# Two MLPs cut into four products that hand over through DRAM, one of them by Strassen's algorithm

## The chip, the cores and the metric

One core of a Trainium2 chip runs the whole program. The metric is the device time of one execution in microseconds (us); three executions of the kernel before took 1062.81, 1064.90 and 1064.33 us, median 1064.33.

## The reference

Decay attention, then an MLP with swish, then an MLP with a leaky ramp, all in float32:

```python
batch, n_heads, seq, head_dim = 4, 8, 576, 64        # q, k, v: float32
scores = q @ k.T / sqrt(D) + cum[..., :, None] - cum[..., None, :]   # cum = cumsum(log f), causal
x = softmax(scores) @ v                              # -> x: 2304 tokens x 512
h = x @ w1_in;  g = h * sigmoid(1.702 * h);  y = g @ w1_out          # 512 -> 2048 -> 512
h = y @ w2_in;  g = max(h, 0) + alpha * min(h, 0);  out = g @ w2_out # 512 -> 2048 -> 512
```

The four weight matrices arrive as float64.

## The kernel before

**One core, one planner.** The kernel first lists its operations with `plan.add` (line 78): the engines that could do one, a duration for each, what it reads and writes, and a priority (a lower number goes first). `plan.run` (line 105) then walks through them in planned time, always takes the operation that can start first (among equals the one of lower priority number), gives it the engine where it ends soonest, and so writes a fixed order for TensorE (PE), VectorE (DVE), ScalarE (ACT), GpSimd (POOL) and the DMA queue on SyncE (SP). On the chip each engine works off its list in that order and waits at semaphores. A `Pool` is a set of buffers; an operation that opens a buffer waits until one is free.

**Precision.** A float32 value is split in two float32r halves, high (`a_copy`, on ACT, else on DVE) and low (`a_sub`, on POOL or DVE). A product of two such values takes three matmuls: high x high, high x low, low x high. A tile of 128 x 512 of a float64 weight becomes a float32 pair in `convert` (line 476): a 512 KB load, two ACT scalings (lines 485 and 486), then on DVE a shift (487), an `or` (490) and an addition (493), and at last the split, one copy on ACT and one subtraction (361). Three raw buffers (`wraw`) and three result buffers (`wc`) serve all weights.

**Attention** runs in 32 units: for each of 4 batches and 4 pairs of heads first the queries 0 to 255, then for all of them the queries 256 to 575. `prep` loads and transposes, `chunk` finds row maxima, `chunk2` makes the scores, the exponentials and the product with v, and writes x, transposed, into a ring `xr` of 768 tokens (line 746). Units 0 to 15 give tokens 0 to 1023, 256 for each four units, and units 16 to 31 the rest, 320 for each four.

**MLP 1, first half (`mlp1a`)** is the filler beside attention. Its priority numbers (1000 and up) stand behind attention's (100 to 131), so PE takes it when attention has nothing ready. It goes over blocks of 256 tokens in the ring, and for each over 8 of the 16 slices of the 2048 hidden columns: `mlp_slot` makes h (12 matmuls of 256 columns, line 759), tanh on ACT (765), the product on DVE (766), the split, and 12 more matmuls (line 801) add the slice to the two PSUM banks of the output. x itself and the partial output go to DRAM (`xscr`, `ypscr`).

**MLP 1, second half, and MLP 2** come after it. Five blocks of 512, 512, 512, 256 and 512 tokens are read back (`load_x`), and for each slice `mlp_slot` makes h (line 759) and 12 matmuls add it up (882 for MLP 1, 911 for MLP 2). Both products of a slice stand side by side in PE's order, so PE has a first product to do while ACT and DVE work on the slice before. The weights of a slice stay in SBUF for all blocks: 8 slots `wA` from the start, 6 slots `wB` in the space of attention once that is over, 2 slots `wC` in the space of `mlp1a`.

Of the kernel before, what the change touches and what calls it, by code (L numbers as in the profile page):

```python
# [9 lines left out]
I32 = mybir.dt.int32  # L10
# [172 lines left out]
def kernel(  # L183
# [24 lines left out]
    NA = 8  # L208
# [4 lines left out]
    NB = NM - NA  # L213
    NB1 = 6
    RING = 768
    BLK = 256
    SPLIT = 256

# [8 lines left out]
    xscr = dram.tile([P, KT, NT], F32, name="xscr")  # L227
    ypscr = dram.tile([P, KT, NT], F32, name="ypscr")
# [4 lines left out]
    def open_region(name, side, closes=()):  # L233
        if name not in region:
            for c in closes:
# [19 lines left out]
    open_region("res", "left")
    open_region("m1a", "left")
    open_region("att", "right")


    wA = sb("res", "wA", NA, [P, 2, 2 * KT, P], F32R)  # L260
    p_raw8 = sb("res", "wraw", 3, [P, 4, P, 2], I32)
    p_wc = sb("res", "wc", 3, [P, 4, P])
    p_xh = sb("m1a", "xh", 3, [P, 2, BLK], F32R)
    p_xl = sb("m1a", "xl", 2, [P, 2, BLK], F32R)
    p_g = {n: sb("m1a", n, 2, [P, BLK], d) for n, d in (("gg", F32), ("gh", F32R), ("gl", F32R))}
    p_yp = sb("m1a", "yp", 1, [P, 2, BLK])
    xr = region["m1a"][1].tile([P, KT, RING], F32, name="xr")
    m1a_pools = [p_xh, p_xl, p_yp, *p_g.values()]
# [703 lines left out]
```

## Time and profile before

| | us |
|---|---|
| median of three executions | 1064.33 (1062.81 to 1064.90) |
| span of the profiled execution, first to last instruction | 1063.1 |
| PE busy with matmuls in it | 1032.3 |
| DVE, ACT, POOL busy | 680.9, 433.3, 129.3 |
| moved by DMA | 86.54 MB, 81 GB/s in the mean |

The profiled execution has no time of its own beside the span; the span is 0.1% under the median. PE's matmuls overlap their neighbours in the records, so a single one reads longer than the step from one start to the next; the same holds for DVE's operations. In the rows, PEld is the loading of PE's weights, and PEclk the clock that was granted to PE as a share of 2.4 GHz.

### The profile page before, as it was taken

What the parts mean: (1) busy time and instruction counts of PE and PEld (TensorE: products, weight loads), DVE (VectorE), ACT (ScalarE), POOL (GpSimd) and SP (SyncE); (2) the same over time, 40 slices, a digit from 0 to 9 for tenths busy, and PEclk for the clock granted to TensorE, in tenths of its full rate; (3) what the DMA queues carried; (4) which work ended last, traced back from release to release, by engine and by line L of the source; (5) the groups of instructions that cost most, each with busy time, mean ns of one, the idle gap of its engine ahead of it and who ended that gap; (6) DMA issues with size and microseconds to landing.
All of it is one profiled execution on the core that took longest, in us unless ns stands there. A gap on an engine that the chain in (4) does not pass through costs nothing.

```text
span 1063.1 us, 17696 instructions
## 1 busy us (share of the span) xinstructions
PE 1032.3 (97%) x6563; PEld 886.8 (83%) x6563; DVE 680.9 (64%) x1523; ACT 433.3 (41%) x970; POOL 129.3 (12%) x202
## 2 busy tenths in 40 slices
PE   5888999999999999999999999999999999999998
PEld 3667888999888989998888988888888888898886
DVE  6879888887888868939953459634343533544433
ACT  4556545555556546748732348301211211211111
POOL 5222312131113010001200101100000000000000
PEclk8789999999999999999999999999999999999999
DMA  5666664332322114616751236300200100010001
GB/s 113 136 164 189 140 135 90 68 75 55 81 44 55 43 33 154 216 47 197 246 152 60 93 106 190 108 1 1 70 1 1 70 1 0 21 40 21 1 1 39
DMA packets 170055, 86.54 MB, mean 81 GB/s; under 512 B 127440, under 2 KB 155280, under 8 KB 169968
## 3 DMA queue, kind: packets, MB, share of 16 engines
q1 hardware_dynamic: 159632, 84.16, 29.1%
q10 hardware_dynamic: 10336, 1.25, 0.7%
q8 instruction: 51, 0.84, 0.3%
q14 instruction: 36, 0.29, 0.1%
HBM read 66.34 MB, written 19.02 MB: 80 GB/s over the span
## 4 chain that ended last, share of the span: by engine, by line
PE 89%; DMA 3%; DVE 3%; POOL 1%; ACT 1%; issue 1%; SPq 0%; ACTq 0%; DVEq 0%; POOLq 0%
PE bk L759 36%; PE bk L911 18%; PE bk L882 9%; PE bk L801 9%; PE bk L667 5%; PE bk L716 4%; PE bk L604 2%; DMA wraw<-in_moe_w_in_dram 2%; PE bk L687 2%; PE bk L693 1%; DMA wraw<-in_moe_w_out_dram 1%; PE bk L630 1%; DMA rq<-in_q_dram 1%; PE bk L597 1%; DVE wraw L490 0%
## 5 line engine op out<-in xcount | busy, mean ns | idle before, releaser
L356 ACT CAST qgh<-qgg 128x512 fp32r<-128x512 f32 (+1 forms) x118 | 68.3, 579 | 332.5 <-DVE qgg L773 297.1
L770 DVE TENSOR_SCALAR qgg<-bk,alpha_sb 128x512 f32<-128x512 f32 (+1 forms) x80 | 55.4, 695 | 164.9 <-PE bk L759 164.9
L759 PE MATMUL bk<-qx,wB 128*128 128x512 f32 (+1 forms) x720 | 155.5, 368 | 0.0
L759 PEld LDWEIGHTS bk<-qx,wB 128*128 128x128 f32 x720 | 126.0, 189 | 22.7
L759 PE MATMUL bk<-xh,wA 128*128 128x256 f32 x576 | 124.1, 295 | 0.0
L361 DVE TENSOR_TENSOR qgl<-qgg,qgh 128x512 fp32r<-128x512 f32 (+1 forms) x117 | 75.9, 650 | 68.8 <-ACT qgh L356 52.2
L759 PE MATMUL bk<-qx,wA 128*128 128x512 f32 (+1 forms) x480 | 103.6, 368 | 0.0
L759 PEld LDWEIGHTS bk<-xh,wA 128*128 128x128 f32 x576 | 96.7, 194 | 7.3 <-issue 3.7
L759 PEld LDWEIGHTS bk<-qx,wA 128*128 128x128 f32 x480 | 84.2, 188 | 15.3
L801 PE MATMUL bk<-gh,wA 128*128 128x256 f32 x576 | 83.7, 289 | 8.1 <-ACT gh L356 8.1
L613 DVE CUSTOM_DVE_ANT_0 bk<-bk,mask 128x512 f32<-128x512 f32 (+3 forms) x160 | 75.5, 491 | 15.5 <-PE bk L604 12.7
L801 PEld LDWEIGHTS bk<-gh,wA 128*128 128x128 f32 x576 | 74.9, 193 | 10.8 <-ACT gh L356 9.1
L759 PE MATMUL bk<-xl,wA 128*128 128x256 f32 x288 | 82.4, 286 | 0.0
L671 ACT ACTIVATE e<-bk 128x320 f32<-128x320 f32 (+3 forms) x224 | 64.9, 364 | 30.8 <-PE bk L667 26.6
L911 PE MATMUL bk<-wA,qgh 128*128 128x512 f32 x288 | 71.9, 389 | 0.0
L911 PEld LDWEIGHTS bk<-wA,qgh 128*128 128x128 f32 x288 | 53.8, 188 | 11.0
L759 PEld LDWEIGHTS bk<-xl,wA 128*128 128x128 f32 x288 | 55.9, 194 | 0.0
L882 PE MATMUL bk<-qgh,wB 128*128 128x512 f32 (+1 forms) x240 | 54.5, 369 | 0.0
L675 POOL TENSOR_SCALAR_AFFINE_SELECT e<-e 128x256 f32<-128x256 f32 (+1 forms) x80 | 34.4, 444 | 162.0 <-ACT e L671 137.0
L911 PE MATMUL bk<-wB,qgh 128*128 128x512 f32 x216 | 54.0, 390 | 0.0
L759 PE MATMUL bk<-qx,wC 128*128 128x512 f32 (+1 forms) x240 | 52.7, 368 | 0.0
L485 ACT ACTIVATE wc<-wraw 128x512 f32<-128x512 f32 x64 | 43.0, 676 | 23.0 <-DMA wraw<-in_moe_w_in_dram 14.5
(156 smaller groups left out, 1991.1 us busy)
## 6 DMA issues: line engine op xcount, KB each, us to landing
wraw<-in_moe_w_in_dram SPq DMA_DIRECT2D x32, 512.0 KB
wraw<-in_moe_w_out_dram SPq DMA_DIRECT2D x32, 512.0 KB
xscr<-xr SPq DMA_DIRECT2D x9, 512.0 KB
ypscr<-yp SPq DMA_DIRECT2D x18, 256.0 KB
rk<-in_k_dram SPq DMA_DIRECT2D x64, 72.0 KB
VR<-in_v_dram SPq DMA_DIRECT2D x32, 128.0 KB
qxb<-xscr SPq DMA_DIRECT2D x16, 256.0 KB
qyp<-ypscr SPq DMA_DIRECT2D x16, 256.0 KB
```

The source lines that it names most:

```text
L356: nc.scalar.copy(dst, src)
L361: E[e].tensor_tensor(dst, a, b, op=ALU.subtract)
L485: plan.add([("ACT", c_act(n))], lambda e: nc.scalar.mul(w.ap, high().bitcast(F32), 2.0 ** -112), [raw], [w], pri)
L613: plan.add([("DVE", c_dve(c1 - c0) + 90.0)], lambda e, pm=pm, c0=c0, c1=c1, mk=mk, m0=m0, col=col: nc.vector.tensor_tensor_reduce(pm.ap[:, ...
L667: nc.tensor.matmul(pss[hh].ap[:w, :m], x.ap[r, a:a + w], y.ap[r, s0 - q0:n], start=i == 0, stop=i == 3)
L671: plan.add([("ACT", c_act(m, True))], lambda e, hh=hh, pss=pss, e32=e32, w=w, m=m: nc.scalar.activation(e32.ap[:w, hh, :m], pss[hh].ap[:w, ...
L716: nc.tensor.matmul(pb[hh].ap[:l.shape[1], s0 - q0:n], l, rhs.ap[:w, hh, :m], start=st, stop=sp, skip_group_check=True,)
L759: nc.tensor.matmul(ph.ap[:, :n], wb.ap[:, a, c, :], x(c), start=(c == 0 and i == 0), stop=(c == KT - 1 and i == 2))
L770: plan.add([("DVE", c_dve(n) + 56)], lambda e: nc.vector.tensor_scalar(g.ap[:, :n], ph.ap[:, :n], 0.0, alpha_sb[:, m:m + 1], op0=ALU.min, ...
L801: nc.tensor.matmul(py[d // 2].ap[:, d % 2 * BLK:(d % 2 + 1) * BLK], W1[m].ap[:, a, KT + d, :], g.ap, start=(m == 0 and i == 0 and a == 0 a ...
L882: nc.tensor.matmul(py[d].ap[:, :n], W1[m].ap[:, a, KT + d, :], g.ap[:, :n], start=(m == NA and i_ == 0 and a == 0), stop=(m == NM - 1 and ...
L911: nc.tensor.matmul(py[t].ap, g.ap[:, t * P:(t + 1) * P], wo[:, a, KT * P:], start=(m == 0 and i_ == 0 and a == 0), stop=(m == NM - 1 and i ...
```

## The change

All of MLP 1's first product now runs beside attention (`gemm1`): blocks of 256 (three) and 384 tokens (four), all 16 slices each, 12 matmuls a slice; h is copied out of PSUM and stored to DRAM (`h1scr`) with no activation. The partial output and the copy of x in DRAM are gone.

The second stage reads h back in tiles of 128 x 512 (`stream`: load, tanh on ACT, product on DVE, split) and multiplies it by `w1_out`; y goes to DRAM. The third stage is MLP 2's first product. `group_x` reads y for 768 tokens as a 2 x 2 grid (two halves of the 512 inputs, two halves of 384 tokens), forms four sums of them and splits seven operands; the weights get the same treatment for each pair of slices (m, m + 8). `pair` then makes seven block products of 6 matmuls of 384 columns, where the plain way has eight; sums of products are made in PSUM by PE, and with three copies on ACT and three additions on DVE a pair. h goes to DRAM (`h2scr`) with no activation. The sums go over three groups of tokens with the first four pairs, then over the three again with the last four. The fourth stage streams h back with the leaky ramp and multiplies by `w2_out`.

SBUF regions are opened in turn: buffers of a later stage wait until all buffers of an earlier one in the same place are released (`order_of`). The 11 first slices of `w1_out` and the stream buffers take the place of attention; the other five and six slots for Strassen weights take the place of stage 1; the operands of stage 3 take the place of `w1_out`.

```diff
+    BLKS = (256, 256, 256, 384, 384, 384, 384)
+    BW = max(BLKS)
+    XH = 384
+    GRP = 2 * XH
+    NPAIR = NM // 2
+    WO0 = 11
...
+    order_of = {
+        "res": ("left", (), ()), "p1": ("left", (), ()), "att": ("right", (), ()),
+        "str": ("right", ("att",), ()), "wo0": ("right", (), ("str",)), "x0": ("right", ("wo0",), ()),
+        "ws": ("left", ("p1",), ()), "wo1": ("left", (), ("ws",)), "x1": ("left", ("wo1",), ()),
+    }
...
+    wA = sb("p1", "wA", NM, [P, 2, KT, P], F32R)
+    p_xh = sb("p1", "xh", 3, [P, 2, BW], F32R)
+    p_xl = sb("p1", "xl", 2, [P, 2, BW], F32R)
+    p_gg = sb("p1", "gg", 3, [P, BW])
...
+    p_str = {n: sb("str", n, w, [P, 512], d, att_pools) for n, w, d in (("qr", 3, F32), ("qg", 2, F32), ("qh", 3, F32R), ("ql", 2, F32R))}
+    p_yo = sb("str", "yo", 2, [P, 512], F32, att_pools)
+    wo = (sb("wo0", "woa", WO0, [P, 2, 512], F32R, att_pools), sb("wo1", "wob", NM - WO0, [P, 2, 512], F32R, p1_pools))
+    wS = sb("ws", "wS", 6, [P, WSLOT], F32R, p1_pools)
+    p_tt = sb("ws", "tt", 1, [P, 4, 2, P], F32, p1_pools)
+    p_ba = sb("x0", "ba", 6, [P, 2, XH], F32, [wo[0]])
+    p_xs = (sb("x0", "xsa", 3, [P, 2, 2, XH], F32R, [wo[0]]), sb("x1", "xsb", 4, [P, 2, 2, XH], F32R, [wo[1]]))
+    p_t = {n: sb("x1", n, 2, [P, XH], F32, [wo[1]]) for n in ("c1", "u2", "c5")}
+    p_go = sb("x1", "go", 4, [P, XH], F32, [wo[1]])
...
+    def gemm1(i, pri, vpri):
+        t0, n = starts[i], BLKS[i]
...
+        for m in range(NM):
+            ph = Buf(ps_h)
+            w = WI[m]
+
+            def hmm(e, ph, w, c0):
+                for c in (c0, c0 + 1):
+                    for j, (a, x) in enumerate(((0, xh), (0, xl), (1, xh))):
+                        nc.tensor.matmul(ph.ap[:, :n], w.ap[:, a, c, :], x[c // 2].ap[:, c % 2, :n], start=(c == 0 and j == 0), stop=(c == KT - 1 and j == 2))
+
+            for c0 in range(0, KT, 2):
+                plan.add([("PE", 6 * c_mm(n))], lambda e, ph=ph, w=w, c0=c0: hmm(e, ph, w, c0), [(w, (0, 0)), (w, (0, 1)), xh[c0 // 2], xl[c0 // 2]], [ph], pri)
+            g = Buf(p_gg)
+            plan.add(a_out(n), lambda e, g=g, ph=ph: copy(e, g.ap[:, :n], ph.ap[:, :n]), [ph], [g], vpri)
+            plan.add(DMA(P * n * 4), lambda e, g=g, m=m: nc.sync.dma_start(h1scr[:, m, t0:t0 + n], g.ap[:, :n]), [g], [(b_g1, (i, m))], vpri)
...
+            for m in range(NM):
+                WI[m] = Buf(wA)
+                pri = A0 + 4 + m * 0.3
+                w = exact(in_rows(w1_in, m), pri, A0 + 1 + m / 2 if m < 4 else None, WLAG)
+                halves(KT * P, lambda w=w: flat(w.ap), [w], lambda m=m: flat(WI[m].ap[:, 0]), lambda m=m: flat(WI[m].ap[:, 1]), WI[m], 0, pri)
...
+    def stream(src, rd, k, t0, n, act, pri):
+        raw, g, h, lo = (Buf(p_str[x]) for x in ("qr", "qg", "qh", "ql"))
+        plan.add(DMA(P * n * 4), lambda e: nc.sync.dma_start(raw.ap[:, :n], src[:, k, t0:t0 + n]), rd, [raw], pri)
+        if act == "swish":
+            plan.add([("ACT", c_act(n))], lambda e: nc.scalar.activation(g.ap[:, :n], raw.ap[:, :n], AF.Tanh, scale=0.851), [raw], [g], pri)
+            plan.add([("DVE", c_dve(n), 0.0, True)], lambda e: nc.vector.scalar_tensor_tensor(
+                g.ap[:, :n], g.ap[:, :n], 1.0, raw.ap[:, :n], op0=ALU.add, op1=ALU.mult
+            ), [raw], [g], pri)
+        else:
+            plan.add([("DVE", c_dve(n, True) + 56, 0.0, True)], lambda e: nc.vector.tensor_scalar(
+                g.ap[:, :n], raw.ap[:, :n], 0.0, alpha_sb[:, k:k + 1], op0=ALU.min, op1=ALU.mult
+            ), [raw, b_alpha], [g], pri)
+            plan.add([("DVE", c_dve(n), 0.0, True)], lambda e: nc.vector.scalar_tensor_tensor(
+                g.ap[:, :n], raw.ap[:, :n], 0.0, g.ap[:, :n], op0=ALU.max, op1=ALU.add
+            ), [raw], [g], pri)
+        plan.add(a_copy(n), lambda e: copy(e, h.ap[:, :n], g.ap[:, :n]), [g], [h], pri)
+        plan.add(a_sub(n), lambda e: sub(e, lo.ap[:, :n], g.ap[:, :n], h.ap[:, :n].bitcast(F32)), [g, h], [lo], pri)
+        return h, lo
...
+    in_turn = blocks[:-2] + [blocks[-1], blocks[-2]]
+    groups = [(t0, GRP) for t0 in range(0, NT, GRP)]
...
+    for i, (t0, n) in enumerate(in_turn):
+        base = 2000.0 + 100 * i
+        py = [Buf(ps_y) for _ in range(KT)]
+        for k in range(NM):
+            h, lo = stream(h1scr, [(b_g1, (j, k)) for j in crossing(t0, n, p1_parts)], k, t0, n, "swish", base + k - 60)
+            last = k == NM - 1
...
+            rw = [(WO[k], (0, 0)), (WO[k], (0, 1))]
+            for ds in ([d] for d in range(KT)) if last else (range(KT),):
+                pd = [py[d] for d in ds]
+                plan.add([("PE", 2 * len(ds) * c_mm(n))], lambda e, ymm=ymm, ds=ds: ymm(e, ds, ((0, 0), (1, 0))), [*rw, h], pd, base + k)
+                plan.add([("PE", len(ds) * c_mm(n))], lambda e, ymm=ymm, ds=ds: ymm(e, ds, ((0, 1),)), [*rw, lo], pd, base + k)
...
+        diff(0, cut(0)[1], cut(0)[0], w)
+        diff(1, cut(2)[1], t_(0), [w[1], (tt, 0)])
+        diff(2, cut(2)[1], cut(0)[1], [w[1]])
+        diff(3, cut(2)[0], t_(1), [w[0], (tt, 1)])
...
+        o = {}
+        o[1] = operand(a["11"], p_xs[0])
+        comb(s1, a["21"], a["22"], ALU.add)
+        comb(s2, s1, a["11"], ALU.subtract)
+        o[6] = operand(s2, p_xs[0])
+        o[2] = operand(a["12"], p_xs[0])
+        o[5] = operand(s1, p_xs[1])
+        comb(a["21"], a["11"], a["21"], ALU.subtract)
+        o[7] = operand(a["21"], p_xs[1])
+        comb(s2, a["12"], s2, ALU.subtract)
+        o[3] = operand(s2, p_xs[1])
+        o[4] = operand(a["22"], p_xs[1])
+        return o
...
+        product(1, x[1], p, ba, True, pri)
+        cp(c1, ba)
+        product(6, x[6], p, bb, True, pri)
+        add(bb, bb, c1)
+        product(2, x[2], p, ba, False, pri)
+        cp(u2, bb)
+        cp(o11, ba, a_out(XH))
+        store(o11, p, gi, 0, t0, vp)
+        product(5, x[5], p, bd, True, pri)
+        cp(c5, bd)
+        product(7, x[7], p, bb, False, pri)
+        add(o22, bb, c5)
+        store(o22, p + NPAIR, gi, 1, t0, vp)
+        product(3, x[3], p, bd, False, pri)
+        add(o12, bd, u2)
+        store(o12, p + NPAIR, gi, 0, t0, vp)
+        product(4, x[4], p, bb, False, pri)
+        cp(o21, bb, a_out(XH))
+        store(o21, p, gi, 1, t0, vp)
...
+    n_it = 0
+    for half in range(2):
+        for gi, (t0, _) in enumerate(groups):
+            base = 6000.0 + 100 * n_it
+            x = group_x(t0, base - 150)
+            for p in range(half * NPAIR // 2, (half + 1) * NPAIR // 2):
+                pair(p, x, gi, t0, base + p)
+            n_it += 1
...
+        if k % 3 == 0:
+            sw = Buf(wS)
+        W2[k] = (sw, k % 3)
+        pri = 8000.0 + k
```

Here `exact` is `convert` without the split, `halves` the split, `a_out` the copy out of PSUM on ACT or DVE, `p_ba`, `p_xs` the buffers of `group_x`, and `ps_t` six PSUM banks, three for a pair.

## Rows read from the trace of the kernel before

**Rows 1.** The page's first part: busy us, share of the span, instructions.

```profile
PE 1032.3 (97%) x6563; PEld 886.8 (83%) x6563; DVE 680.9 (64%) x1523; ACT 433.3 (41%) x970; POOL 129.3 (12%) x202
```

**Rows 2.** Stretches, all engines: length, busy us (instructions), PEclk, DMA share, GB/s.

```profile
0.00:125.00 125.00, 100.24 (x789) 80.32 (x789) 101.67 (x320) 71.20 (x173) 42.44 (x89) 0.86 0.63 149
125.00:407.00 282.00, 281.14 (x2499) 250.66 (x2495) 228.75 (x605) 149.74 (x403) 57.54 (x91) 1.00 0.32 68
407.00:467.30 60.30, 60.11 (x500) 59.91 (x500) 46.88 (x100) 39.60 (x88) 0.74 (x1) 1.00 0.55 175
467.30:680.00 212.70, 212.70 (x1028) 179.49 (x1028) 150.41 (x260) 113.82 (x203) 23.23 (x16) 1.00 0.46 145
680.00:1058.20 378.20, 378.12 (x1758) 316.47 (x1756) 153.23 (x241) 58.44 (x104) 5.35 (x5) 1.00 0.05 17
1058.20:1063.10 4.90, 0.00 (x0) 0.00 (x0) 0.00 (x0) 0.54 (x1) 0.00 (x0) 0.93 0.65 200
```

**Rows 3.** The chain that ended last, 420 to 530 us: start, us, what.

```profile
433.41 5.22 DMA wraw<-in_moe_w_in_dram
...
444.25 8.64 PE bk L759 x72
...
512.35 9.52 PE bk L759 x42
```

**Rows 4.** Waits of PE, 0 to 125 us: total us, times, longest.

```profile
PE bk L801 <- ACT gh L356: 7.9, 4, 4.1
```

**Rows 5.** Stretches, line 746 alone: DVE's writes into the ring.

```profile
0.00:226.00 226.00, 10.49 (x24) 0.92 0.55 125
```

**Rows 6.** Stretches, line 801 alone: PE, PEld.

```profile
0.00:226.00 226.00, 43.91 (x288) 38.20 (x288) 0.92 0.55 125
0.00:407.00 407.00, 84.81 (x583) 75.30 (x584) 0.96 0.41 93
```

**Rows 7.** Stretches, line 759 alone: PE, PEld.

```profile
0.00:226.00 226.00, 51.34 (x336) 44.86 (x336) 0.92 0.55 125
0.00:407.00 407.00, 97.24 (x648) 84.67 (x648) 0.96 0.41 93
```

**Rows 8.** Groups by line and shape: busy us, mean ns, idle before.

```profile
L485 ACT ACTIVATE wc<-wraw 128x512 f32<-128x512 f32 x64 | 43.0, 676 | 23.0 <-DMA wraw<-in_moe_w_in_dram 14.5 <-DMA wraw<-in_moe_w_out_dram 6.5 <-DVE wc L487 1.0
...
L766 DVE SCALAR_TENSOR_TENSOR gg<-gg,bk 128x256 f32<-128x256 f32 x72 | 29.7, 412 | 5.3 <-ACT gg L765 4.9
...
L765 ACT ACTIVATE gg<-bk 128x256 f32<-128x256 f32 x72 | 27.5, 382 | 32.8 <-PE bk L759 19.5 <-DVE gl L361 10.3 <-POOL gl L361 2.2
```

**Rows 9.** Instructions in order of time, DVE, 500 to 502 us: start, us.

```profile
499.98 0.69 DVE L490 SCALAR_TENSOR_TENSOR wraw<-wraw 128x512 int32<-128x512 int32 x1
500.58 0.69 DVE L361 TENSOR_TENSOR wA<-wc,wA 128x512 fp32r<-128x512 f32 x1
501.18 0.69 DVE L493 CUSTOM_DVE_ANT_0 wc<-wraw,wc 128x1024 uint16<-128x1024 uint16 x1
501.78 0.43 DVE L487 TENSOR_SCALAR wc<-wc 128x512 int32<-128x512 int32 x1
502.12 0.69 DVE L490 SCALAR_TENSOR_TENSOR wraw<-wraw 128x512 int32<-128x512 int32 x1
```

**Rows 10.** Instructions in order of time, all engines, 557 to 560 us.

```profile
557.55 0.60 ACT L765 ACTIVATE qgg<-bk 128x512 f32<-128x512 f32 x1 [3.98 <-PE bk L759]
...
559.56 0.69 DVE L361 TENSOR_TENSOR qgl<-qgg,qgh 128x512 fp32r<-128x512 f32 x1 [0.69 <-ACT qgh L356]
```

**Rows 11.** A stretch of 55 us, all engines, columns as in rows 2.

```profile
475.00:530.00 55.00, 55.00 (x244) 45.27 (x243) 54.29 (x92) 43.73 (x78) 9.32 (x6) 1.00 0.65 205
```

**Rows 12.** The page's second part: what all DMAs moved.

```profile
DMA packets 170055, 86.54 MB, mean 81 GB/s; under 512 B 127440, under 2 KB 155280, under 8 KB 169968
```

**Rows 13.** Instructions in order of time, the end of the span.

```profile
1057.18 0.33 SPq L931 DMA_DIRECT2D out_dram<-qyp  x1
...
1059.45 0.40 SPq L931 DMA_DIRECT2D out_dram<-qxb  x1
```

More of the change, by code (lines that the diff above doesn't have):

```diff
@@ L780, in mlp1a @@
[L780 to L784 removed]
+    b_g1, b_y1, b_g2 = Buf(), Buf(), Buf()
+    WI = {}
+    starts = [sum(BLKS[:i]) for i in range(len(BLKS))]
+    def gemm1(i, pri, vpri):
+        t0, n = starts[i], BLKS[i]
+        r0 = t0 % RING
+        xb = xr[:, :, r0:r0 + n]
+        cols = [j % (RING // 64) for j in range(t0 // 64, (t0 + n) // 64)]
@@ L830, with advance @@
+    done = {"i": 0}
+    def advance(t):
+        while done["i"] < len(BLKS) and starts[done["i"]] + BLKS[done["i"]] <= t:
+            gemm1(done["i"], 1000.0 + done["i"], -1.0)
+            done["i"] += 1
     seq = [(b, hp, q0, q1) for q0, q1 in ((0, SPLIT), (SPLIT, S)) for b in range(B) for hp in range(NP)]
@@ L840 @@
             chunk2(x)
-            advance(t, 0)
+            advance(t)
     for x, t in pend:
         chunk2(x)
-        advance(t, 0)
-    for m in range(NA, NM):
-        W1[m] = weight(wB if m < NA + NB1 else wC, w1_in, w1_out, m, 2000.0 + m)
-    blocks = []
-    for n in (512, 512, 512, NT % 512, 512):
-        blocks.append((sum(x[1] for x in blocks), n))
-    nx = {"i": 0}
+        advance(t)
     def row_of(x):
@@ new lines, in crossing @@
+    def crossing(t0, n, parts):
+        return [i for i, (a, w) in enumerate(parts) if a < t0 + n and t0 < a + w]
+    p1_parts = list(zip(starts, BLKS))
+    blocks = [(512 * i, min(512, NT - 512 * i)) for i in range((NT + 511) // 512)]
+    in_turn = blocks[:-2] + [blocks[-1], blocks[-2]]
+    groups = [(t0, GRP) for t0 in range(0, NT, GRP)]
+    WO = {}
+    for k in range(NM):
+        WO[k] = wb = Buf(wo[k // WO0])
+        pri = 1500.0 + k
+        w = exact(out_rows(w1_out, k), pri)
+        halves(KT * P, lambda w=w: flat(w.ap), [w], lambda wb=wb: wb.ap[:, 0], lambda wb=wb: wb.ap[:, 1], wb, 0, pri)
@@ new lines, with product, mm @@
+    TIDX = {1: 0, 2: 1, 3: 2, 4: 6, 5: 3, 6: 4, 7: 5}
+    def product(j, x, p, out, st, pri):
+        def mm(e):
+            t = TIDX[j]
+            w = TS[p].ap.rearrange("p (a q c n) -> p a q c n", a=2, q=7, c=2)
+            for c in range(2):
+                for i, (a, b) in enumerate(((0, 0), (0, 1), (1, 0))):
+                    nc.tensor.matmul(
+                        out.ap[:, :XH], w[:, a, t, c, :], x.ap[:, b, c, :],
+                        start=(st and c == 0 and i == 0), stop=(c == 1 and i == 2), skip_group_check=True,
+                    )
+        k = PART[TIDX[j]]
+        plan.add([("PE", 6 * c_mm(XH))], mm, [(TS[p], (k, 0)), (TS[p], (k, 1)), (x, (0, 0)), (x, (0, 1))], [out], pri)
```

287 lines of the change are left out of this document (123 added, 164 removed).

## The prediction

> **What bounds the kernel now.** The page's first part puts PE busy for 1032.3 of 1063.1 us [rows 1]; DVE, the next, has 64%. A busy PE can hide waits, so the second look is the span cut into stretches [rows 2]. The reader is to see three things there. Up to 125 us PE is busy for 100.24 us: 24.8 us are idle, and its clock is granted at 0.86. From 125 us, through the rest of attention (to about 407 us), the rest of MLP 1's first half (to 467.3 us) and everything behind it, PE is idle for 1.1 us in 933 us. The end without PE takes 4.9 us.
>
> The third look is the chain that ended last. In a full stretch it gives the true step of a matmul: 72 of 256 columns took 8.64 us, so 120.0 ns; 42 of 512 columns took 9.52 us, so 226.7 ns [rows 3]. That is a line, N / 2.4 + 13.3 ns, and 384 columns, which the kernel before does not have, come to 173.3 ns between the two. With these steps the products from 467.3 us on need 768 x 226.7 + 192 x 120 = 197.1 us (second half of MLP 1), 197.1 us (MLP 2, first product) and 864 x 226.7 = 195.9 us (second), together 590.1 us; the stretch is 590.9 us long. So the kernel is bound by PE's count of columns, and any change is read as: matmuls removed, less the places where PE has nothing ready.
>
> **The change part by part: what PE no longer does.** Stage 1: before, 9 blocks x 8 slices x 24 matmuls of 256, 1728 x 120.0 = 207.4 us. After, 192 matmuls for each of three blocks of 256 and four of 384: 192 x (3 x 120.0 + 4 x 173.3) = 202.2 us: -5.2 us, the fixed 13.3 ns of fewer matmuls. Stages 2 and 4 have the old shapes: 0. Stage 3: 3 groups x 8 pairs x 7 products x 6 = 1008 matmuls of 384, 174.7 us for 197.1: -22.4 us. In all -27.6 us.
>
> The Trainium skill has another fixed part: in "TensorE: Matmul & The Clock Gate", "Wait — 56ns, not 53.3ns?", the step is N / 2.4 GHz plus about 2.5 ns. By that the sum would be -1.0 for stage 1 and -22.9 us for stage 3, -23.9 us and 1054.4 us at the end. The chain here reads 120.0 and 226.7 ns, so the measurement decides.
>
> **Stage 1.** What it adds on PE is nothing; the question is whether attention always finds filler beside it. Before, when unit 20 was done (24 writes into the ring, 226 us), PE had done 288 + 336 filler matmuls [rows 5 to 7], 74.9 us. After, until then only three blocks are there, 576 x 120 = 69.1 us. PE would lack 5.8 us of work. Against it, DVE loses 29.7 us of products and the subtractions behind them, and ACT trades 27.5 us of tanh and as much of copies for 112 copies out of PSUM, 0.38 us for 256 columns by line 765 and for 384 some 0.5, between that and line 485's 0.676 for 512 [rows 8]; two PSUM banks that the output held are free. Attention may reach unit 20 earlier by that. In the first 125 us PE waited 7.9 us for the split of an activation [rows 4]; that wait is gone, but the same place then waits for weights, which come through the same loads and as many conversions (16 tiles either way). I take +3 for missing filler (bounds 0 and 8), -2 for the early wait (bounds -8 and 0): +1 us. At attention's end 1728 - 583 - 648 = 497 filler matmuls, 60 us, were left [rows 6, 7]; after it is at least the last block, 33 us, in which the first 11 slices of w1_out are converted.
>
> The queue: 27 stores leave SP, 112 come in, each waiting for a copy out of PSUM; at about 0.4 us to issue [rows 13] 45 us of SP's 400. Behind a late store stand loads of q, k and v, which run two units ahead. DMA in all goes from 86.5 MB [rows 12] by -18.9 (x and partial output, out and back) +75.5 (h, 2304 x 2048 x 4 bytes, twice out and back) +4.7 (y read twice) to about 148 MB. The first 125 us have a DMA share of 0.63 already [rows 2]; beside attention the stores come to +9.4 MB in 407 us, 23 GB/s, by the ratio of rows 11 (205 GB/s at 0.65) a share of 0.07. I cost it at nothing; it shows if the share nears 1.
>
> **Stage 2.** Now each slice is 12 matmuls, 2.72 us, and PE has no other product to turn to: behind the matmul that waits for `qh` stand only later slices, which come through the same buffers. Uncontended, the way from tanh to the low half took 2.70 us (557.55 to 560.25, [rows 10]); two `qg` buffers make that 1.35 us a slice. Beside it run conversions: five slices of w1_out (waiting until the buffers of stage 1 are released) and six of eight Strassen weights. DVE's real step is what the starts say, 0.60 us for 512 columns with two inputs and 0.34 for the shift, not the 0.69 in the records [rows 9]. A slice takes 1.20 us of DVE; a tile's conversion 1.54, its split 0.60. A Strassen pair: 2 x 1.54, four differences of 256 columns at about 0.34, subtractions of 512, 256 and 1024 columns at 0.60, 0.34 and 1.2, 6.6 us. The stage has 72 x 1.20 + 5 x 2.14 + 6 x 6.6 = 137 us of DVE for 197 us of PE; ACT, with two scalings of 0.676 us a tile, has less. The nearest row is the stretch from 475 to 530 us: DVE busy 54.29 of 55.00 us with conversions, PE without a gap [rows 11]. But there PE had two products to choose from. So I take +2 us for the start of the stage (bounds 0 and 5) and +3 for the conversions beside the streams (bounds 0 and 34, below).
>
> **Into stage 3 and through it.** The loads of y for group 0 wait for the buffers of slice 10 of the last block: 5 x 2.72 = 13.6 us before the stage's end. 1.57 MB at the 205 GB/s of rows 11 need 7.7 us, and a 512 KB load took 5.2 us to land [rows 3]; three operands are split by then, four after the last slice, each by one copy and one subtraction of 768 columns, which PE covers with 3.1 us of the first three products: +2 us (bounds 0 and 5). Inside a pair product 2 waits for copy c1 under cover of product 6 (1.04 us against some 0.5 us of copy and a hand-over), product 7 for an addition and a copy under products 2 and 5, product 4 for an addition under product 3; three more banks let the next pair in. In the 29 us of four pairs DVE has 11 operations of 768 columns at 0.9 us and 12 of 384 at 0.45 (from rows 9, by columns), 15 us, and ACT 7 copies of 768 at 0.9 and 20 of 384 at 0.5, 16 us. +2 us (bounds 0 and 8).
>
> **Stage 4 and the end.** Two of the six slots for w2_out come free halfway through stage 3, the others 22, 15, 7 and 0 us before its end, so ten conversions crowd around the border: +2 us (bounds 0 and 6). At the end there are two output buffers where four served. Before, the last three copies did not wait; the last DMA was issued at 1059.45 and landed by 1063.1, 3.2 us after its 0.40 us of issue [rows 13]. After, the third copy waits for the first store and the fourth for the second: about 1060.4 and 1061 us in these times, then 0.6 us, issue and 3.2 us: +2 us (bounds 0 and 3.5).
>
> **The sum.** -27.6 + 1 + 2 + 3 + 2 + 2 + 2 + 2 = -13.6 us. Against the profiled execution's 1063.1 us that is 1049.5; against the median of 1064.33, 0.1% above that execution, 1050.7 us, which I forecast.
>
> **Rivals.**
> *Everything hides.* The five inner borders cost nothing, the early wait goes by 3 us or more, only the tail stays: -27.6 - 2 + 2 us, 1036.7 us. For it: PE lost 1.1 us in 933 under the same planner. Against it: that order always held a second product.
> *The streams of stage 2 set its pace (slower).* Place: PE's wait for `qh` or `ql` in stage 2, with DVE or ACT ahead of it at Strassen conversions. Two buffers keep up while the way from tanh to low half stays under 5.44 us, so each of its four steps may wait 0.68 us, a bit more than one conversion operation. If it is 6.4 us in all 72 slices, a slice takes 3.2 us: +34 us in place of 3, 1050.7 + 31 = 1081.7 us. It turns the change into a loss from 2.95 us a slice (72 x 0.23 = 16.6 us). For it: conversions are taken whenever an engine is free, and rows 11 show DVE full by them. Against it: DVE's 137 us for the stage.
> *Filler runs out in earnest.* Blocks of 384 come later than blocks of 256, and with attention no faster PE lacks its 8 us at each of two borders, the DRAM traffic delays loads: +17 us in stage 1, 1066 us. For it: rows 5 to 7. Against it: the lack at unit 20 is 5.8 us, and each block behind it brings 33 us of filler.
>
> **How the numbers follow.** The forecast (1040 to 1062) has 0.55, everything hidden 0.21, the slow streams 0.19, the filler 0.05. A difference of 0.2%, 2.1 us, is about what a measurement of this kernel can tell. Of the slow streams 0.04 ends within it and 0.15 above; of the filler 0.02 and, below it, 0.03. Faster: 0.55 + 0.21 + 0.03 = 0.79; same 0.06; slower 0.15. The likeliest case alone spans 1040 to 1062 us. The range goes from 1034 (all hidden, with a little more of the early wait) to 1068 us, into the slow streams, and leaves out some 0.14 above and 0.04 below.
>
> **What would show it.** 1008 matmuls in stage 3 at steps of 173 ns and a stage of 177 us; stage 2 at 197 to 202 us; attention's end with 33 to 80 us of filler left; PE's waits in stage 2 named for `qh` and `ql`, around 5 us in all; a last DMA that lands some 7 us after the last matmul. Wrong it would be if PE were idle for over 15 us in one of the stages, or if a 384-column step were not near 173 ns.

## The result, and the profile after

The changed kernel took 1049.41 us (median of four executions, 1046.55 to 1054.58) beside 1063.57 for the kernel before: ratio 0.9871, 95% interval 0.9834 to 0.9907. With five further executions the median of nine is 1049.0. The forecast was 1050.7. The profiled execution is the longest of the nine, 1054.58 us with a span of 1052.8, so each stage is also read from later profiles.

Page of the changed kernel, first part, and what its DMAs moved (answers to [rows 1] and [rows 12]):

```profile
PE 1005.4 (95%) x6227; PEld 887.9 (84%) x6227; DVE 751.8 (71%) x1595; ACT 542.2 (52%) x1152; POOL 106.1 (10%) x174
...
DMA packets 211293, 147.94 MB, mean 141 GB/s; under 512 B 132320, under 2 KB 186272, under 8 KB 211200
```

Its stretches, columns as in [rows 2]: the first 125 us, the rest of stage 1, stage 2, stage 3, stage 4, the tail.

```profile
0.00:125.00 125.00, 93.99 (x767) 74.83 (x769) 97.81 (x304) 69.60 (x172) 36.51 (x82) 0.88 0.64 150
125.00:470.33 345.33, 340.93 (x2641) 309.72 (x2640) 232.95 (x578) 181.40 (x453) 46.90 (x77) 0.99 0.42 111
470.33:666.10 195.77, 195.52 (x953) 165.47 (x952) 151.61 (x269) 127.96 (x228) 0.00 (x0) 1.00 0.53 164
666.10:852.03 185.93, 180.57 (x1018) 177.62 (x1017) 136.97 (x213) 110.45 (x209) 19.97 (x13) 0.99 0.60 195
852.03:1046.89 194.86, 194.35 (x857) 160.29 (x855) 132.43 (x233) 51.64 (x90) 2.67 (x3) 1.00 0.37 110
1046.89:1052.80 5.91, 0.03 (x1) 0.00 (x0) 0.00 (x0) 1.17 (x2) 0.00 (x0) 0.92 0.48 145
```

Where PE was idle before, it is idle still, and more: 31.0 us of the first 125 for 24.8 [rows 2]. New are 4.4 idle us in the rest of stage 1 (1.05 before) and 5.4 in stage 3 (180.57 busy of 185.93). Those of stage 1 lie early; behind 170 us it is full:

```profile
170.00:470.33 300.33, 299.48 (x2273) 273.91 (x2272) 202.34 (x479) 160.81 (x391) 35.62 (x59) 1.00 0.40 111
```

Stages 2 and 4, whose streams I feared, are full. The chain that ended last (start, us, what) has 300 matmuls of 384 columns in one piece, and PE's instructions within it show six at a time:

```profile
671.50 52.38 PE bk L967 x300
```

```profile
673.69 1.20 PE L967 MATMUL bk<-xsa,wS 128*128 128x384 f32 x6
674.73 1.20 PE L967 MATMUL bk<-xsb,wS 128*128 128x384 f32 x6
675.77 1.20 PE L967 MATMUL bk<-xsa,wS 128*128 128x384 f32 x6
```

From start to start six take 1.04 us, so 173.3 ns a step, as I had it between the two steps of [rows 3]. 52.38 / 300 = 174.6 ns is a mean with small gaps in it.

PE's waits in the first 125 us (line and what it waited for; total us, times, longest), the answer to [rows 4]:

```profile
PE bk L680 <- ACT DQ L653: 9.5, 5, 5.3
...
PE bk L790 <- ACT wA L361: 4.5, 2, 2.4
...
PE bk L790 <- DVE wA L366: 1.3, 4, 0.7
```

The wait of 7.9 us for a split activation is gone; 5.8 us for weights stand in its place. The wait for `DQ`, a scaling on ACT in the attention, has grown. Before it was:

```profile
PE bk L667 <- ACT DQ L640: 2.8, 3, 2.0
```

What held the longest of the five, in order of time at 55 to 61 us:

```profile
55.52 0.50 SPq L796 DMA_DIRECT2D h1scr<-gg  x1
...
56.58 0.48 SPq L796 DMA_DIRECT2D h1scr<-gg  x1
...
60.10 0.37 ACT L361 COPY gg<-bk 128x256 f32<-128x256 f32 x1 [3.83 <-DMA h1scr<-gg]
60.37 0.38 ACT L653 ACTIVATE DQ<-bk 67x256 fp32r<-67x256 f32 x1
...
60.80 0.58 PE L680 MATMUL bk<-DQ,DK 64*128 64x256 f32 x2 [5.27 <-ACT DQ L653]
```

The copy of a new h slice waits 3.83 us until an older store has landed and its `gg` buffer is free. `DQ` stands behind the copy in ACT's order, and PE waits 5.27 us for `DQ`. An issue is 0.5 us on SP's row; the store itself is not in that record. The Trainium skill ("Perfetto Trace Analysis", "Per-instruction lifecycle: what the profiler-reported window actually captures") says that of a DMA the data movement lies outside the reported window, and that DVE and ACT work strictly in order. The rows agree: a store of 0.5 us on SP's row holds the copy for 3.83 us, and `DQ` starts only behind it.

### The profile page after: what moved, and what is told of

Same layout as the page of the kernel before. It is cut to its first block, busy times and chain, and to the rows that moved or that the text cites. A ratio compares the mean times of both kernels' runs of the same rounds, so it can differ in the third digit from the quotient of the medians.

```text
span 1052.8 us, 18331 instructions
## 1 busy us (share of the span) xinstructions
PE 1005.4 (95%) x6227; PEld 887.9 (84%) x6227; DVE 751.8 (71%) x1595; ACT 542.2 (52%) x1152; POOL 106.1 (10%) x174
## 4 chain that ended last, share of the span: by engine, by line
PE 69%; DVE 9%; DMA 3%; issue 2%; ACT 1%; SPq 0%; DVEq 0%; ACTq 0%
PE bk L1045 18%; PE bk L790 16%; PE bk L967 13%; PE bk L877 11%; PE bk L680 4%; PE bk L729 4%; DVE ql L366 1%; PE bk L617 1%; DVE qg L836 1%; DMA ba<-y1scr 1%; PE bk L706 1%; DVE wS L366 1%; DVE wc L500 1%; DMA wraw<-in_moe_w_in_dram 1%; PE bk L700 1%
## 5 line engine op out<-in xcount | busy, mean ns | idle before, releaser
L790 PE MATMUL bk<-xh,wA 128*128 128x384 f32 (+1 forms) x896 | 228.7, 326 | 6.1 <-ACT wA L361 4.5
L361 ACT CAST qh<-qg 128x512 fp32r<-128x512 f32 (+1 forms) x159 | 91.9, 579 | 169.3 <-DVE qg L843 115.8
L366 DVE TENSOR_TENSOR ql<-qg,qh 128x512 fp32r<-128x512 f32 (+1 forms) x158 | 100.5, 637 | 101.9 <-PE bk L877 48.6
L1045 PE MATMUL bk<-wS,qh 128*128 128x512 f32 x576 | 145.9, 389 | 0.5 <-ACT qh L361 0.5
L790 PE MATMUL bk<-xl,wA 128*128 128x384 f32 (+1 forms) x448 | 142.0, 317 | 0.8 <-DVE xl L366 0.8
L1045 PEld LDWEIGHTS bk<-wS,qh 128*128 128x128 f32 x576 | 108.0, 188 | 23.3 <-ACT qh L361 0.9
L967 PE MATMUL bk<-xsb,wS 128*128 128x384 f32 x576 | 110.1, 339 | 5.4 <-DVE go L989 4.0
L967 PEld LDWEIGHTS bk<-xsb,wS 128*128 128x128 f32 x576 | 101.6, 190 | 7.9 <-DVE go L989 5.3
L877 PE MATMUL bk<-qh,woa 128*128 128x512 f32 (+1 forms) x440 | 99.4, 368 | 0.0
L967 PE MATMUL bk<-xsa,wS 128*128 128x384 f32 x432 | 82.5, 334 | 0.0
```

What stands on the lines that cost most here:

```text
L361: nc.scalar.copy(dst, src)
L366: E[e].tensor_tensor(dst, a, b, op=ALU.subtract)
L790: nc.tensor.matmul(ph.ap[:, :n], w.ap[:, a, c, :], x[c // 2].ap[:, c % 2, :n], start=(c == 0 and j == 0), stop=(c == KT - 1 and j == 2))
L877: nc.tensor.matmul(py[d].ap[:, :n], w[:, a, d * P:(d + 1) * P], (lo if x else h).ap[:, :n], start=(k == 0 and (a, x) == (0, 0)), stop=(k = ...
L967: nc.tensor.matmul(out.ap[:, :XH], w[:, a, t, c, :], x.ap[:, b, c, :], start=(st and c == 0 and i == 0), stop=(c == 1 and i == 2), skip_gr ...
L1045: nc.tensor.matmul(py[t].ap, (lo if x else h).ap[:, t * P:(t + 1) * P], w[:, a], start=(k == 0 and (a, x) == (0, 0)), stop=(k == NM - 1 an ...
```

## The experiments

Differences are against the 1049.0 us of the changed kernel. Executions of one kernel differ by 2 to 9 us in all of them, and by 4 to 7 us in the kernel before; the first experiment shows where a part of it is from.

**The same kernel again.**

> The changed kernel once more. Its four executions so far run from 1046.55 to 1054.58 us, and the profiled one is the longest of them. If the loss of stage 1 in that profile (PE idle for 31.0 us in the first 125 us against 24.8 before, DQ waits of 9.5 us) belongs to the kernel, a second profile shows it again, at 29 to 33 us. If it came by chance from the timing of DMAs in that one execution, the second profile has 25 to 28 us there and a span near 1047.

1049.02 us (1046.91 to 1052.52), ratio 0.9858 (0.9837 to 0.9880). Idle in the first 125 us: 28.0 us, between both cases, and `DQ` 9.6 us again. Stage 1 ended at 470.33 once more. Six profiles (this pair and the four runs below marked *) have the same order of work through stage 1. It ended at 466.83, 467.23 and 467.23 us in three and at 470.33, 470.33 and 471.03 in the others. Two of them side by side, by the starts of `DQ` on ACT:

| | 16th `DQ` | 17th | last | stage 1 ends |
|---|---|---|---|---|
| changed kernel | 151.74 | 169.44 | 391.38 | 470.33 |
| eight products* | 150.50 | 166.18 | 388.13 | 466.83 |

From the 17th to the last `DQ` the two run in step, 3.3 us apart. So this scatter is decided before 170 us. In the rows just ahead of the 17th, ACT's copy of v waits for a late load (2.6 us in the changed kernel, 2.1 in the other) with the exponentials behind it, and PE waits for those. What carries the difference, by the rows, is PE's clock. The second measurement and the run on the tail below (first and second line) start that copy of v at 156.54 and 156.37 us and are 3.1 us apart at the 17th `DQ` (169.23 and 166.11). Their stretches from 125 to 170 us:

```profile
125.00:170.00 45.00, 40.92 (x359) 35.18 (x356) 30.22 (x96) 20.34 (x61) 11.27 (x18) 0.92 0.55 110
```

```profile
125.00:170.00 45.00, 41.52 (x399) 35.66 (x398) 32.00 (x106) 22.14 (x66) 11.30 (x18) 1.00 0.58 116
```

PE is idle for 4.1 and 3.5 us, but its clock is granted at 0.92 in the one and 1.00 in the other. In all three that end late it is 0.92, in the three that end early 0.96, 0.96 and 1.00. In the changed kernel the row of PE after that wait, and the stretch behind it at 0.50 of 2.4 GHz:

```profile
157.68 0.52 PE L680 MATMUL bk<-QH,KH 64*128 64x192 f32 x1 [2.32 <-ACT e L684]
```

```profile
158.00:162.00 4.00, 4.00 (x25) 3.54 (x24) 2.29 (x8) 2.61 (x7) 1.36 (x4) 0.50 0.71 131
```

So a wait of some 2 us can be paid twice, once in idle time and once in slower matmuls behind it; after 2.09 us in the run on the tail it was not.

**Strassen's price and gain*.**

```diff
         product(1, x[1], p, ba, True, pri)
+        product(1, x[1], p, ba, True, pri)
```

> Strassen undone in its price alone: the first block product of every pair is issued twice, the second time over the first (start=True), so stage 3 has eight products where the changed kernel has seven; everything else and the result stay. 24 pairs x 6 matmuls x 174.6 ns = 25.1 us. Theory (PE's columns set the time, what else stage 3 does is hidden): +24 to +26 us on the changed kernel, about 1073 us. Rival (stage 3 is partly set by the additions, the copies and the loads of y on DVE, ACT and DMA, so PE has slack there): +10 to +20 us, since the second product fills the 9 us that PE lost in stage 3.

1070.36 us: +21.4, between the two theories; ratio to the kernel before 1.006 (1.004 to 1.0079), so with the eighth product in place nothing of the gain is left. Stage 3 of this kernel:

```profile
662.10:867.03 204.93, 203.92 (x1166) 202.10 (x1165) 139.86 (x222) 110.73 (x206) 15.12 (x9) 1.00 0.55 177
```

Take the 1152 matmuls of eight products at the mean of 174.6 ns (201.1 us) and the 12 of stage 4 that run inside it at 226.7 (2.7 us) off the 204.93: 1.1 us lost. The same sum for seven products, with 8 of stage 4, is 185.93 - 176.0 - 1.8 = 8.1 us lost, and 5.5 in the second profile (183.33 us). So leaving out one product of eight takes 25.1 us of columns away, and PE gives some 4 to 7 us of them back (8.1 or 5.5 less 1.1 by the stage; 25.1 - 21.4 = 3.7 by the medians). That fits copies, additions and loads having an eighth less PE time to hide behind; that this is all of it is not shown.

**A fourth buffer for the stores of stage 1.**

```diff
-    p_gg = sb("p1", "gg", 3, [P, BW])
+    p_gg = sb("p1", "gg", 4, [P, BW])
```

> One more buffer (four for three) between the copy out of PSUM and the h1 store of stage 1. Theory: stage 1 lost about 6 us of its gain because the copy waits on ACT for an old store to land (3.8 us at 55.6 us of the profile) and attention's DQ scaling stands behind it in ACT's order (PE waits 5.3 us): PE's idle time in the first 125 us falls from 31.0 us to 25 to 28, the time by 3 to 5 us. Rival (the loss belongs to SP's queue, full of issues and late for q, k and v, or to the weights of the first block): idle time 30 us or more, no gain over 1 us.

1044.84 us (1043.49 to 1046.39), -4.2, as expected; but not where expected. No copy waits for a store any more, yet PE's idle time in the first 125 us is 33.0 us; between 125 us and the end of stage 1 (466.13) it is 1.3 us for 4.4, and the granted clock from 125 to 170 us is 1.00 for 0.92. One profile does not prove that place, as the scatter above is as large; and the interval (0.9798 to 0.9838) just meets that of the changed kernel's second measurement (0.9837 to 0.9880).

**Stores of two slices.**

```diff
-    p_gg = sb("p1", "gg", 3, [P, BW])
+    p_gg = sb("p1", "gg", 2, [P, 2, BW])
...
+            if m % 2:
+                plan.add(DMA(2 * P * n * 4), lambda e, g=g, m=m: nc.sync.dma_start(h1scr[:, m - 1:m + 1, t0:t0 + n], g.ap[:, :, :n]), [g], [(b_g1, (i, m - 1)), (b_g1, (i, m))], vpri)
```

> The h1 stores of stage 1 go out for two slices at a time: 56 DMAs where the changed kernel issues 112, the same bytes, two buffers of two slices (four slices in flight where three were). Theory (the copies wait for buffers whose stores are late, and SP's list is full of issues in the first 175 us): as with the fourth buffer, no wait of a copy for a store is left, and SP has 24 issues fewer in its full stretch, so 1043 to 1046 us against 1049 for the changed kernel. Rival (the issues themselves set it, not the buffer): below 1043, clearly faster than the fourth buffer's 1044.84. Second rival (each store waits for two slices, so buffers come back later): 1047 or more.

1043.73 us (1040.78 to 1046.86), -5.3: within the first theory and, at 0.9806 (0.9783 to 0.9829), clear of the changed kernel, but not to be told from the fourth buffer. ACT's waits for DMAs up to 180 us, first the changed kernel, then this one:

```profile
ACT DQ L653 <- DMA rq<-in_q_dram: 4.8, 1, 4.8
...
ACT gg L361 <- DMA h1scr<-gg: 3.8, 1, 3.8
...
ACT VH L361 <- DMA VR<-in_v_dram: 2.6, 1, 2.6
ACT VH L361 <- DMA rq<-in_q_dram: 2.5, 1, 2.5
```

```profile
ACT VH L361 <- DMA VR<-in_v_dram: 0.7, 1, 0.7
ACT VH L361 <- DMA rk<-in_k_dram: 0.5, 1, 0.5
```

Left out are the weight loads (16.5 and 19.4 us together) and one wait of `xr` of 5.5 and 5.6 us. The waits for stores are gone, and those for v are 1.2 us for 5.1. The bytes are the same, and the DMA share of the first 125 us is higher, 0.68 for 0.64, so bandwidth was hardly the lack. The granted clock from 125 to 170 us is 1.00. Stage 1 ended at 460.83 us, and at 462.73 and 463.33 in the two joined kernels below, 5.5 to 8 us before the mean of the six (468.8).

**Every store twice.**

```diff
+            plan.add(DMA(P * n * 4), lambda e, g=g, m=m: nc.sync.dma_start(h1b[:, m, t0:t0 + n], g.ap[:, :n]), [g], (), vpri)
```

> Every h1 store of stage 1 is issued twice, the second time into a DRAM tensor that nobody reads: 112 DMAs and 18.9 MB more in 470 us. Theory (stores cost stage 1 by their buffers and their place in SP's list): each buffer is held longer and loads of q, k, v stand behind more issues, stage 1 ends 4 to 12 us later, 1053 to 1061 us. Rival (what I predicted: queue and DMA traffic of the stores cost nothing): within 2 us of the changed kernel's 1049.

1052.89 us (1051.05 to 1053.55), +3.9: a shade under the theory's range and over the rival's. Copies wait for stores eight times, 10.7 us in all, for twice and 6.1 us. But the end of stage 1, expected 4 to 12 us later, is 471.7 us with 12 matmuls of stage 2 done for 8, 2 us behind the mean of the six, and the interval (0.9873 to 0.9906) just meets that of the second measurement. With half the issues 5.3 us less, with twice as many 3.9 more: the stores have a price, which the first of the two shows and the second bears out, and I had put it at nothing.

**Nine blocks of 256.**

```diff
-    BLKS = (256, 256, 256, 384, 384, 384, 384)
+    BLKS = (256,) * 9
```

> Stage 1 goes over nine blocks of 256 tokens in place of three of 256 and four of 384: 1728 matmuls for 1344, 144 stores for 112. Theory (the block size is worth its fixed part, 207.4 - 202.2 = 5.2 us, and filler did not run out with 384): +5 to +8 us, the part above 5.2 for 32 more stores, 1054 to 1057 us. Rival (blocks of 384 come too late as filler beside attention, which cost what their matmuls gained): within 2 us of the changed kernel, 1047 to 1051.

1058.28 us (1056.01 to 1062.44), +9.3. More than the 5.2 us of matmuls; with 32 more stores the copies' waits for them are 10.5 us up to 470 us, for 6.1. The rival, larger blocks too late as filler, is out.

**A slower stream in stage 2.**

```diff
+        if act == "swish":
+            plan.add([("DVE", c_dve(n), 0.0, True)], lambda e: sub("DVE", lo.ap[:, :n], g.ap[:, :n], h.ap[:, :n].bitcast(F32)), [g, h], [lo], pri)
```

> The subtraction for the low half is done twice in every slice of stage 2, on DVE: 72 x 0.60 us by the starts, 43 us of DVE more in a stage where DVE had 152 us in records (about 137 by starts) of 196. Theory (the way from load to low half lies in the shadow of 2.72 us of PE a slice with two buffers, and stays there): stage 2 at most 5 us longer, 1049 to 1054 us. Rival (the streams were near the pace that two buffers hold, 2.95 us a slice was my break-even): stage 2 longer by 15 us or more, 1064 us and up.

1056.22 us (1052.70 to 1060.45), +7.2, just outside the theory and far from the rival. Stage 2 of it, and PE's waits there:

```profile
466.93:669.70 202.77, 198.95 (x953) 166.55 (x952) 188.16 (x344) 128.74 (x229) 0.00 (x0) 0.99 0.52 157
```

```profile
PE bk L879 <- DVE ql L366: 3.6, 4, 1.6
```

43 us more on DVE cost 7 us here, where DVE is busy for 188 of 203 us in records. PE is idle for 3.8 of them; part of the rest is matmuls that took longer: behind the first of these waits its clock falls, to 0.95 in the mean from 467 to 500 us. So some 36 of the 43 us found room: the rival's mechanism exists, and the changed kernel stands that far from it.

**Later sums of y on DVE*.**

```diff
+YLAG = 4000.0
...
-            plan.add(DMA(P * 2 * XH * 4), lambda e, x=a[q], c0=c0, s0=s0: nc.sync.dma_start(x.ap, y1scr[:, c0:c0 + 2, s0:s0 + XH]), rd, [a[q]], pri)
+            plan.add(DMA(P * 2 * XH * 4), lambda e, x=a[q], c0=c0, s0=s0: nc.sync.dma_start(x.ap, y1scr[:, c0:c0 + 2, s0:s0 + XH]), rd, [a[q]], pri, YLAG)
```

> The plan counts 4 us more for every load of y in stage 3, so DVE's list takes the sums of the next group's operands later, behind the pair additions that PE waits for; buffers, loads and work are the same. Theory (head of the line on DVE: sums that wait for a late y load, 3.2 us at 796 us, hold up pair additions, PE waits 2.2 us behind them): PE's waits for additions of stage 3 fall from 4.0 us to under 1.5, stage 3 from 183.9 to 179 to 181 us, the time by 3 to 5 us. Rival (y itself is late because its loads share the DMAs with w2_out at 276 GB/s, or is issued late because buffers are not free): PE then waits for the operands instead, and the time stays within 1 us.

1047.30 us (1045.71 to 1048.05): -1.7, less than the theory and more than the rival, and within the scatter (0.9838, 0.9819 to 0.9858). What it acts on, in the changed kernel at 788 to 800 us, DVE and PE in order of time:

```profile
788.85 0.90 SPq L933 DMA_DIRECT2D ba<-y1scr  x2
...
796.09 2.82 DVE L938 TENSOR_TENSOR ba<-ba,ba 128x768 f32<-128x768 f32 x3 [3.21 <-DMA ba<-y1scr]
798.83 0.55 DVE L989 TENSOR_TENSOR go<-bk,c 128x384 f32<-128x384 f32 x1
...
799.44 2.93 PE L967 MATMUL bk<-xsb,wS 128*128 128x384 f32 x8 [2.18 <-DVE go L989]
```

The sums (line 938) wait 3.21 us for a load that took 7 us, take 2.8 us, and the addition that PE needs comes after them. PE's eight matmuls behind that wait take 2.93 us, where eight steps are 1.4: from 799.5 to 802.5 us its clock is granted at 0.50. With the longer lag in the plan no such wait is among DVE's longest in stage 3, but another has come:

```profile
DVE go L990 <- DMA h2scr<-go: 4.6, 2, 2.7
```

The additions now wait for their own output buffers, whose stores land late. PE still waits 2.8 us for additions, for 4.0 and 2.4 in the changed kernel's two profiles. Stage 3 is 183.03 us; the expected 179 to 181 did not come.

**w2_out loads after the last y load*.**

```diff
-        w = exact(out_rows(w2_out, k), pri)
+        w = exact(out_rows(w2_out, k), pri, rd=[b_x5])
```

> The loads of the first w2_out slices, which in the changed kernel run from halfway through stage 3 beside the loads of y, wait until the last group's loads of y have landed. Theory (late y loads and h2 stores at the two borders behind the middle of stage 3 come from sharing the DMAs with 512 KB weight loads, 276 GB/s at 775 to 800 us): additions no longer wait there, PE's waits in stage 3 fall from 3 to 5 us to under 1.5, stage 3 to 179.5 to 181 us, and stage 4 pays 0 to 2 us for later weights. Rival (loads are issued late for want of buffers, whoever shares the DMAs): waits as before, the time within 1.5 us of 1049 or longer.

`b_x5` is what the last group's loads of y write. 1048.18 us (1043.69 to 1052.42): no change that can be told; three executions lie at 1043.7 to 1045.4 us and three at 1051.0 to 1052.4, so the median says little. But the waits changed place. PE waited for additions 0.3 us in stage 3, for 4.0 and 2.4 in the changed kernel's two profiles; near the end of stage 3 stands a wait for a copy:

```profile
834.41 4.96 PE L969 MATMUL bk<-xsb,wS 128*128 128x384 f32 x18 [1.80 <-ACT u L361]
```

Line 969 is the pair product here. The loads of w2_out go out from 788 to 841 us, where the changed kernel has two at 565 to 570, ten from 740 to 785 and four from 835. The DMA rate was 255 GB/s at 775 to 800 us and 238 at 825 to 850, for 276 and 194: the crowd is moved. That fits the theory's cause, but stage 3, 182.27 us, missed the expected 179.5 to 181, and runs without this edit have it as short (182.4 us with two-slice stores). That a gain was made and given back is not shown.

**The tail, and a later place for additions*.**

```diff
-            yo = Buf(p_yo)
+            spare = i == len(in_turn) - 1 and t < 2
+            yo = Buf(p_wc if spare else p_yo)
...
+ALAG = 600.0
...
-            plan.add([("DVE", c_dve(XH))], lambda e: nc.vector.tensor_tensor(dst.ap[:, :XH], x.ap[:, :XH], y.ap, op=ALU.add), [x, y], [dst], vp)
+            plan.add([("DVE", c_dve(XH))], lambda e: nc.vector.tensor_tensor(dst.ap[:, :XH], x.ap[:, :XH], y.ap, op=ALU.add), [x, y], [dst], vp, ALAG)
```

> Two edits that lie in different stretches and are read there. Tail: the first two of the last four output tiles leave through buffers of the weight conversion, so no copy waits for a store. In all profiles so far the stretch from the last matmul to the end takes 5.91 us (4.9 before); theory: 4.7 to 5.0 us; rival (the last store's own landing sets it): 5.8 to 6. Stage 3: the plan counts 0.6 us more behind every pair addition, so that TensorE's list puts other products between an addition and the product that waits for it. Theory (the cover of one product, 1.05 us, is too short for addition and hand-over when DVE is a little late): stage 3 with 7 products, 178.3 us of matmuls with the ten of stage 4 in it, falls from 182 to 186 us to 179.5 to 181. Rival (DVE is late by 3 us and more at the group borders, where loads of y and stores of h land late): no change within 1 us of 182.4. Time 1 to 5 us under the changed kernel's 1049.

1045.71 us (1041.77 to 1050.66), -3.3, as a time not clear of the changed kernel (0.9832, 0.9805 to 0.9859). Stage 3 and the tail:

```profile
662.50:844.53 182.03, 179.22 (x1022) 176.98 (x1021) 140.49 (x220) 109.21 (x207) 13.33 (x10) 1.00 0.61 200
...
1038.49:1043.10 4.61, 0.04 (x1) 0.00 (x0) 0.00 (x0) 0.59 (x1) 0.00 (x0) 1.00 0.63 190
```

The tail falls from 5.91 to 4.61 us: settled. Stage 3 holds 12 matmuls of stage 4, so 182.03 - 176.0 - 2.7 = 3.3 us are lost, fewer than in the nine profiles above with seven products and without this edit (3.6 to 8.1), but hardly outside them: not settled.

**All three, and all three with earlier w2_out loads.**

```diff
-        x = group_x(t0, base - 150, n_it == 5)
+        x = group_x(t0, base - 150, n_it == 4)
```

> Stores of two slices in stage 1, 0.6 us more behind a pair addition in the plan, and two more output buffers at the end, together. If the three losses are separate terms of one sum bound by TensorE, the gains add: two-slice stores 1049.2 - 1043.7 = 5.5 us, the other two together 1049.2 - 1045.7 = 3.5 us, so about 1040 us (1038 to 1042), stage 1 ending at 461 to 464 us and the stretch after the last matmul at 4.6 us. If they hide one another (each draws on the same late DMAs), 1043 to 1045.

> The same three edits, and the first w2_out loads wait until the y loads of the last group but one have landed. Theory (the crowd of conversions and weight loads is moved, not removed, as when they waited for the last group's loads): within 1.5 us of the three edits alone. Rival (in the middle between the two places both y loads and conversions find room): stage 3 under 180.5 us with its ten matmuls of stage 4, 1 to 3 us below the three edits alone.

The diff is the second kernel's against the edit of w2_out above. 1043.60 us (1040.84 to 1044.47), ratio to the kernel before 0.9795 (0.9778 to 0.9812), and 1041.90 us (1040.54 to 1046.34), 0.9792 (0.9771 to 0.9813). The gains did not add: 1040 was expected of the first. Stage 1 ended at 462.73 and the tail was 4.51 us, both as expected; stage 3 lost 3.9 us and, in the second, 2.9. The second is 1.7 us under the first, just past the theory's 1.5, but its stage 3 of 181.7 us misses the rival's 180.5, and the intervals are nearly the same: neither is shown. Both beat the changed kernel by intervals that do not meet those of its second measurement, and neither can be told from the two-slice stores alone (0.9806, 0.9783 to 0.9829).

## Why the prediction came out, step by step

The sum was within 0.2% of the result, but several of its terms were not, and part of that closeness is luck. All figures are the changed kernel's two profiles.

- **PE's columns, -27.6 us: right.** 1344 and 1008 matmuls, a step of 173.3 ns as forecast. Undoing either half gave it back: 21.4 us for the eighth product (25.1 us of columns), 9.3 for the blocks of 256 (5.2 of columns). By the Trainium skill's fixed part of 2.5 ns ("TensorE: Matmul & The Clock Gate", "Wait — 56ns, not 53.3ns?") an estimate of this step is 162.5 ns; the trace has 173.3.
- **Stage 1, +1 us: too small.** It ended at 470.33 us in both profiles, 3.0 us after the kernel before, with 1.85 us of stage 2 already done. Against 467.3 - 5.2 that is a loss of 6.4 us; where it ended at 466.8 to 467.2, of about 3. The step that failed is "I cost it at nothing; it shows if the share nears 1". The share did stay at 0.64. What I left out is that a store holds one of three buffers until it lands, and that a copy waits for the buffer in ACT's order with attention behind it; the rows at 55 to 61 us show that once. That SP's list delays loads even where the DMAs have room is likely, but the runs do not separate it from the buffers. I left out the clock too: from 125 to 170 us PE is idle for 3.6 us, where it was never idle before, and its clock is granted at 0.92 for 1.00. The other two terms of stage 1 were off as well. The early wait, -2, became a loss. Missing filler, +3, was nothing: behind 170 us PE is idle for 0.9 us, and the chain has 384 of the 1344 matmuls behind attention's end at 401.45 us, 67 us. Of the signs of being wrong one was badly put: PE is idle for over 15 us in stage 1, 35.4 us, but it was for 25.8 before.
- **Stage 2, +5 us: too much.** 195.8 and 196.4 us, with the 1.85 pulled forward 197.6 and 198.2, for 197.1 of matmuls: +0.5 to +1.1. PE waited 0.3 and 0.8 us for `ql`. The second product that PE no longer has to turn to was not needed.
- **Stage 3 with the border to it, +4 us: too small.** 8.1 and 5.5 us lost beside the mean step and 1.3 in the small gaps of that step, 9.4 and 6.8. I placed them at the outer border and inside a pair; most lie in the fourth and fifth of the six groups, 754 to 800 us, where y loads, h2 stores and w2_out loads meet. Part of the first profile's is the clock at 0.50 behind its longest wait.
- **Stage 4 and the tail, +4 us: too much.** 194.86 us, and the eight matmuls done in stage 3 (1.8 us) make 196.7 for 195.9: +0.8. The third output copy waited 1.51 us for a store; tail 5.91 for 4.90, so +1.0.

With -27.6 + 6.4 + 0.5 + 9.4 + 0.8 + 1.0 the first profile comes to 1053.6 us (span 1052.8), the second to 1051.6 (1050.8). The terms too small (stage 1 by 2 to 5 us, stage 3 by 3 to 5) and those too large (stage 2 by 4, stage 4 with the tail by 2) cancelled in part, and the median lies below both profiles: that is the luck in the 0.2%. *Everything hides* (1036.7) failed at stages 1 and 3; the slow streams did not occur, though the run with one more subtraction shows the start of them.

Open: two-slice stores end stage 1 at 460.83 - 1.85, which is 3.1 us better than 467.3 - 5.2, although PE's idle time up to there (28.2 us) is more than before (25.8 up to 467.3). By the rows of single lines up to there it is mostly attention's own matmuls: those of line 680, the scores, are busy for 69.7 us there and were for 72.6 before (line 667), those of line 729, products with v, for 50.5 and 53.1 (line 716). Why is open.

## What to carry to other kernels

- When work is moved to DRAM, count its stores by the buffers they hold until they land and by what stands behind the waiting copy and the issue; the DMA share, 0.64 here, showed neither. Fewer, larger stores or one more buffer gave 4 to 5 us of 1049 here.
- Removing an eighth of the bounding engine's work also removes an eighth of the cover: here 4 to 7 of 25.1 us came back as waits. Repeating the removed work with everything else in place measures that in one run.
- Moving a crowd of loads away from one wait emptied that wait here, but gave no gain that could be told, and PE waited for a copy at the new place.
- Read the granted clock behind a wait before pricing the wait by its idle time: behind waits of some 2 us it was 0.50 for a few us at 158 and at 799.5 us.

## What was not expected of the hardware

- One fixed order of instructions ended stage 1 at two places, 466.8 to 467.2 and 470.3 to 471.0 us (three profiles each), with a granted clock of 0.92 from 125 to 170 us in the late ones and 0.96 to 1.00 in the early ones; behind that the compared profiles ran in step, so two profiles can differ by 3 us in a stretch that no edit touched.
- Doubling the bytes and issues of a store stream (18.9 MB more in 470 us) cost 3.9 us in the medians, just at the edge of what can be told; the DMA share from 125 us to the end of stage 1 rose from 0.42 to 0.57.
